# One attention tile's P.V on column strips of the array, and O transposed by VectorE

## The chip, the cores and the metric

The kernel runs on one core of one Trainium2 chip. Its time is the device time of one execution in microseconds (us). Three executions of the kernel before took 279.31, 279.51 and 279.59 us; their median, 279.51 us, is the time before. One execution was profiled: it took 279.08 us, of which its instructions span 277.4 us. TensorE, VectorE, ScalarE, GpSimd and the queue that issues most transfers, SyncE, appear in the profile as PE (weight loads as PEld), DVE, ACT, POOL and SP.

## What is computed

One transformer block with modulation by a condition `c`: sliding-window attention (16 heads of 28, window 256), then a gated MLP whose gate mixes along the sequence with the 2048x2048 matrix `w_sp`. All tensors are bfloat16, 2048 tokens of width 448. `ln` is layernorm without scale.

```python
mod = silu(c) @ w_mod                      # six vectors of 448: sa, ca, ga, sb, cb, gb
h = ln(x) * (1 + ca) + sa
q, k, v = split(h @ wqkv)                  # 16 heads of 28
s = q @ k.T * 28**-0.5                     # per head
s = where(0 <= i - j < 256, s, -1e9)       # query i, key j
x = x + ga * ((softmax(s) @ v) @ wo)
h = ln(x) * (1 + cb) + sb
z = gelu(h @ w_in); z1, z2 = z[:, :896], ln(z[:, 896:])
x = x + gb * ((z1 * (w_sp @ z2 + b_sp)) @ w_out)
```

## The kernel before

**How the order is made.** The program is a list of operations, each with its dependencies, made by the calls of `add`, `pe`, `dve`, `act`, `pool`, `turn` and `load`. Which engine does an operation, and in which order, is written out in the string `ORDER` (lines 19 to 74): a word such as `399.a.4.0` is operation 399, on ACT, with the buffers 4 and 0. Letters are p, a, v, g, s for PE, ACT, DVE, POOL and SP. `Sched` sets semaphore waits for what crosses engines (`waits`) and emits each engine's list (`emit`). Every engine works its own list strictly in order, so an operation that waits holds up all that stands behind it on its engine; SP's list holds nearly all DMA issues. A `Hold` is one use of a buffer; its `until` list says what has to be done before the buffer's next use.

**Stages.** (1) Loads, modulation vectors, norm and Q/K/V projections of the first block of four tiles (a tile is 128 tokens; blocks `tb` 0 to 3). Heads are padded from 28 to 32, so a group `qi` of four heads fills 128 partitions; Q and K lie transposed (`qT`, `KT`), V as `Vaug[128 keys, tile, head, 32]` with a column of ones at 28, so that P.V gives the sum of P as its column 28. (2) Attention of 16 query tiles `j`, each in two halves (two groups of four heads), with the projections of blocks 1 to 3 in between. (3) The projection by `w_in` with gelu; `w_sp` is read transposed meanwhile by DMA (`wspA`, `wspB`). (4) The product with `w_sp` and the output projection.

**Attention of a half, for tiles from 2 on.** The window of a query tile covers three key tiles: the oldest, the middle, the newest. Of the oldest and the newest each query needs a part. `S` (line 858) makes 36 small products with K=32, four heads at a time on four row strips of the array: first with 128 columns of weights, then sixteen with 64. They fill four PSUM banks (0 to 3), of which each head's 512 columns hold the middle tile of the first group and the two masked parts of both groups. `S mid` (line 867) is one product of 512 columns for the second group's middle tile, against `QBD`, Q spread block-diagonally (bank 5). ACT takes the exponential of both into `PW` (line 819: 2048 columns, then 512; five buffers). DVE multiplies with the 0/1 mask, once per group, from `PW` into another tile, `PT` (line 874). P.V (line 901) takes 128 keys x 128 queries of P as weights and 32 columns of V as moving operand: per half 24 products, into bank 4, where O has queries on partitions. Tiles 0 and 1 have one and two key tiles, go through lines 832 and 894, and use the same line 901.

**After P.V of a tile.** DVE takes the reciprocal of column 28 (line 915) and multiplies O with it into `o_sb` (line 917). SP issues a DMA that transposes `o_sb` into `hT` (`turn`, line 468). PE multiplies with `wo_g` (line 926), DVE adds to x (line 931), then `stats` (lines 592 to 600, the last step on POOL) and `norm` (lines 606 to 620: on POOL or DVE, with a small POOL operation, line 614, in front), a second DMA transposition, and the modulation (lines 949 and 951). The projection by `w_in` (lines 1011 and 1032) waits for these and for the last P.V.

Of the kernel before, what the change touches and what calls it, by code (L numbers as in the profile page):

```python
# [19 lines left out]
2.a 24.v 33.g 0.s 25.v 26.v 27.v 36.g 37.g 3.a 1.s 34.g 4.a 31.g 28.v 5.s 35.g 8.a 29.v 38.g 6.s 9.a 7.s 43.a 39.g 53.p.1 54.p.2 55.p.3 44.p.0 130.v  # L20
128.v 131.v 129.v 132.g 45.a 46.a 56.p.4 57.p.5 58.p.6 59.p.7 60.p.2 52.p.1 139.v 137.v 140.v 138.v 133.g 134.v 141.v 136.a.0 142.g 135.a.1 143.v
120.v 145.v.2 108.v 107.v 67.p.3 146.p.2 144.a.3 68.p.0 69.p.4 147.p 150.p.3 40.g 123.g 121.g 122.v 148.v 149.v 151.p 152.a 48.a 70.p.0 71.p.0
154.p.4.5.6.7 155.p 156.p 153.a 158.p 125.g 42.g 160.p 159.p 157.p 162.a 164.a 32.g 41.g 124.g 47.v 10.s 11.s 14.s 127.g 126.v 191.v 192.v 187.v 30.v
49.g 50.g 13.s 15.s 16.s 12.s 161.a 169.p.0 170.a 171.p.1 172.a 346.p.0 347.a.0 163.v 185.v 189.v 186.v 188.v 190.v 51.v 175.p.7 173.p.6 112.p.0
114.p.1 193.g 194.g 199.g 201.g 197.g 200.g.0 195.g 176.v 202.v.1 198.v.2 113.v 196.g.3 350.v 174.a 352.p.0 353.a.1 181.p.7 203.p.0 371.p.0 166.s
167.s 165.s 168.s 17.s 348.v 115.v 206.p.1 177.p.6 204.v 205.v 207.v 109.p.0 372.a.2 373.a 182.a 208.a 378.p.0 379.a.3 380.a 239.v 241.v 243.v 237.v
244.v 110.v 238.v 20.s 19.s 18.s 240.v 242.v 354.v 111.v 178.v 179.p.7 183.p.1 211.p.0 184.v 293.v 356.v 180.v 349.p.0 398.p.0 212.a 351.p 355.p
215.p.1 357.p 400.p.0 209.p.0 399.a.4.0 381.v 291.v 216.v 406.p.0 210.a 245.g 246.g 251.g 252.v.0 358.v 359.v.0 376.v 374.v 253.g 249.g 254.g.1 403.v
221.p.1 213.p.0 383.v 214.v 402.v 294.v 375.p.0 377.p 407.a.5.1 401.a 427.p.0 222.a 408.p.0 382.p 223.p.0 225.p.1 428.a.6.2 435.p.0 409.a 411.v
429.p.0 384.p 258.s 118.g 247.g 250.g.2 256.s 257.s 248.g.3 255.s 262.g 259.g 226.a 436.a.0.3 292.v 224.v 295.v 385.v 386.v.1 229.p.0 227.p.1 404.p.0  # L30
410.v 297.v 228.v 430.a 456.p.0 230.a 457.a.1.4 360.s 218.s 219.s 220.s 217.s 432.v 261.v 260.v 437.p.0 233.p.0 231.p.1 405.p 412.p 296.v 232.v 438.a
234.a 464.p.0 413.p 275.p.1 263.p.0 458.p.0 465.a.2.0 431.v 298.v 116.g 299.g 119.g 300.g 117.g 307.g 305.g 306.g.0 301.g 308.g.1 302.g.2 439.v 414.v
415.v.2 264.v 469.v 440.v 460.v 468.v 276.a 459.a 485.p.0 486.a.3.1 433.p.0 265.p.1 434.p 441.p 466.p.0 493.p.0 266.a 467.a 303.g 304.g.3 442.p
235.p.0 489.v 443.v 444.v.0 494.a.4.2 461.v 487.p.0 269.p.1 514.p.0 236.a 488.a 462.p.0 277.p.0 463.p 470.p 471.p 495.p.0 515.a.5.3 522.p.0 270.v
490.v 497.v 416.s 387.s 472.v 473.v.2 278.a 267.p.1 268.v 498.v 491.p.0 492.p 361.p.0 362.v 523.a.6.4 526.v 363.v 496.a 543.p.0 544.a.0.0 516.p.0
388.p.1 499.p 279.p.0 389.v 548.v 547.v 517.a 280.a 551.p.0 552.a.1.1 500.p 417.p.1 524.p.0 281.p.0 501.v 518.v 418.v 502.v.1 527.v 519.v 525.a 282.a
# [229 lines left out]
def bass_adaLN_cond__sliding_block__mixer_gmlp__prompt_kernel(  # L266
# [15 lines left out]
    NT = S // 128  # L282
    DC = 4
    DP = 512
    NB4 = NT // 4
    EPS = 1e-5
    SCALE = float(DH) ** -0.5
    NPT = 7
    NPW = 5

    ARENA_BYTES = 207 * 1024
    arena = nc.alloc_sbuf_tensor("arena", [128, ARENA_BYTES // 2], BF16)
    base = nc.lookup_mloc(arena).addr
    cursor = [0]
# [860 lines left out]
```

## Time and profile before

| | us |
|---|---|
| median of three executions | 279.51 (279.31 to 279.59) |
| the profiled execution | 279.08, of which 277.4 is its span |
| start to the first exponential of 2048 columns | 0 to 30.10 |
| from there to the end of the last exponential | 30.10 to 109.95 |
| from there to the first product with `w_sp` | 109.95 to 156.60 |
| the rest | 156.60 to 277.40 |

A table of busy times by stretch gives, per engine, the time in which it had an instruction under way, with the number of instructions in brackets. "idle before" in a group of instructions is the time the engine waited in front of them, and the name behind the arrow is what ended the wait. Matmuls overlap, so the mean duration of one is no price; the distance between starts is. The granted TensorE clock is 1.0 in every stretch.

### The profile page before, as it was taken

What the parts mean: (1) busy time and instruction counts of PE and PEld (TensorE: products, weight loads), DVE (VectorE), ACT (ScalarE), POOL (GpSimd) and SP (SyncE); (2) the same over time, 40 slices, a digit from 0 to 9 for tenths busy, and PEclk for the clock granted to TensorE, in tenths of its full rate; (3) what the DMA queues carried; (4) which work ended last, traced back from release to release, by engine and by line L of the source; (5) the groups of instructions that cost most, each with busy time, mean ns of one, the idle gap of its engine ahead of it and who ended that gap; (6) DMA issues with size and microseconds to landing.
All of it is one profiled execution on the core that took longest, in us unless ns stands there. A gap on an engine that the chain in (4) does not pass through costs nothing.

```text
span 277.4 us, 7383 instructions
## 1 busy us (share of the span) xinstructions
PE 266.4 (96%) x3198; PEld 140.8 (51%) x3225; DVE 164.4 (59%) x364; ACT 128.2 (46%) x154; POOL 127.2 (46%) x191
## 2 busy tenths in 40 slices
PE   4999999999999999999999999999999999999995
PEld 1636466656576766444444444444444444444452
DVE  5679999989989999679798300300320042025434
ACT  2587999999999999577676600000000000000000
POOL 6831826914725669884949000600571065334110
PEclk9999999999999999999999999999999999999999
DMA  7966142145993666834999999100000000001113
GB/s 208 304 170 205 23 91 47 21 80 96 121 225 79 80 80 97 194 77 83 190 176 205 206 197 187 35 0 0 0 2 0 0 0 2 0 0 56 62 50 99
DMA packets 65843, 26.01 MB, mean 94 GB/s; under 512 B 56466, under 2 KB 64723, under 8 KB 65811
## 3 DMA queue, kind: packets, MB, share of 16 engines
q1 hardware_dynamic: 65168, 24.68, 43.4%
q10 hardware_dynamic: 642, 0.86, 1.1%
q8 instruction: 25, 0.41, 0.6%
q14 instruction: 8, 0.06, 0.1%
HBM read 9.01 MB, written 1.84 MB: 39 GB/s over the span
## 4 chain that ended last, share of the span: by engine, by line
PE 82%; DVE 8%; DMA 4%; POOL 3%; issue 1%; ACT 0%; ACTq 0%; SPq 0%; POOLq 0%
PE ps L1055 35%; PE ps L1032 8%; PE ps L1072 7%; PE ps L1011 6%; PE ps L708 5%; PE ps L901 5%; PE ps L858 3%; DMA hT<-xn 3%; PE ps L926 3%; PE ps L756 3%; PE ps L867 2%; DVE st_all L592 2%; PE ps L557 1%; DMA c_row<-in_c_dram 1%; PE ps L696 1%; POOL hT L951 1%
## 5 line engine op out<-in xcount | busy, mean ns | idle before, releaser
L819 ACT ACTIVATE PW<-ps 128x2048 bf16<-128x2048 f32 (+1 forms) x56 | 67.4, 1242 | 2.9 <-PE ps L867 1.1
L1059 DVE TENSOR_TENSOR tmpg<-ps,bsp_bc 128x512 bf16<-128x512 f32 x28 | 19.1, 691 | 83.4 <-PE ps L1055 69.3
L1062 POOL TENSOR_TENSOR z1T<-tmpg,z1T 128x512 bf16<-128x512 bf16 x28 | 31.9, 1153 | 79.3 <-DVE tmpg L1059 79.3
L1055 PE MATMUL ps<-wspB,z 128*128 128x512 bf16 x218 | 49.5, 379 | 0.3
L1055 PE MATMUL ps<-wspA,z 128*128 128x512 bf16 x220 | 48.8, 379 | 0.3 <-issue 0.2
L874 DVE TENSOR_TENSOR PT<-PW,mask 128x1024 bf16<-128x1024 bf16 x56 | 38.9, 721 | 0.7 <-ACT PW L819 0.7
L1055 PEld LDWEIGHTS ps<-wspA,z 128*128 128x128 bf16 x224 | 21.8, 98 | 26.6 <-issue 0.4
L1055 PEld LDWEIGHTS ps<-wspB,z 128*128 128x128 bf16 x224 | 21.9, 98 | 26.2
L600 POOL TENSOR_TENSOR rs_all<-ve_all,neghalf 128x1 f32<-128x1 f32 (+2 forms) x37 | 23.6, 645 | 3.7 <-DVE ve_all L597 3.0
L1011 PE MATMUL ps<-w_in,hT 64*128 64x448 bf16 x224 | 23.0, 349 | 1.2 <-DVE hT L951 0.6
L901 PE MATMUL ps<-Vaug,PT 128*128 128x32 bf16 x496 | 24.1, 177 | 0.1
L901 PEld LDWEIGHTS ps<-Vaug,PT 128*128 128x128 bf16 x496 | 21.8, 96 | 4.0 <-DVE PT L894 0.6
L1032 PE MATMUL ps<-hT,w_in 64*128 64x512 bf16 x196 | 22.5, 376 | 0.0
L1072 PE MATMUL ps<-w_out_g,z1T 128*128 128x448 bf16 x112 | 22.2, 352 | 0.0
L708 PE MATMUL ps<-hT,WQK 128*128 128x512 bf16 x80 | 20.5, 379 | 1.3 <-issue 0.4
L616 POOL TENSOR_SCALAR xn<-x_sb,rs_all,ve_all 128x448 bf16<-128x448 bf16 x21 | 18.1, 863 | 7.0 <-DMA hT<-xn 6.4
L901 PE MATMUL ps<-Vaug,PW 128*128 128x32 bf16 x224 | 20.1, 176 | 0.0
L592 DVE BATCH_NORM_STATS2 st_all<-x_sb 128x6 f32<-128x448 bf16 x32 | 18.9, 610 | 1.6 <-DMA x_sb<-in_A_x_dram 1.5
L592 DVE BATCH_NORM_STATS2 st_all<-z 128x6 f32<-128x448 bf16 x32 | 18.3, 607 | 1.7 <-ACT z L1018 1.7
L901 PEld LDWEIGHTS ps<-Vaug,PW 128*128 128x128 bf16 x224 | 17.6, 96 | 1.9
L597 POOL TENSOR_SCALAR ve_all<-mv_all 128x1 f32<-128x1 f32 (+2 forms) x20 | 6.6, 334 | 25.1 <-DVE mv_all L595 21.5
L1018 ACT ACTIVATE z<-ps 128x896 bf16<-128x896 f32 x16 | 14.1, 916 | 7.8 <-PE ps L1011 6.8
(101 smaller groups left out, 343.9 us busy)
## 6 DMA issues: line engine op xcount, KB each, us to landing
out_dram<-fin SPq DMA_DIRECT2D x16, 112.0 KB, 1.7
x_sb<-in_A_x_dram SPq DMA_DIRECT2D x3, 448.0 KB, 3.9
wmod<-in_w_mod_dram SPq DMA_DIRECT2D x1, 1344.0 KB, 9.5
w_in<-in_B_w_in_dram SPq DMA_DIRECT2D x1, 1344.0 KB, 8.2
QBD<-qT SPq DMA_DIRECT2D x16, 64.0 KB, 2.5
w_out_g<-in_B_w_out_dram SPq DMA_DIRECT2D x1, 784.0 KB, 4.9
bsp_bc<-in_B_b_sp_dram SPq DMA_DIRECT2D x1, 512.0 KB, 5.0
x_sb<-in_A_x_dram SPq DMA_DIRECT2D x2, 224.0 KB, 4.2
```

Source lines behind the costliest of these rows:

```text
L592: st = [dve(0.62 if True else 0, lambda e, t=t, ci=ci, s=s: e.bn_stats(st_all[:, slot, t, ci, :], s()), deps(t), prio) for ci, s in enumer ...
L600: rs = pool(0.53 + 0.15 * len(tiles), lambda e: e.tensor_tensor(rs_all[:, slot, a:b], ve_all[:, slot, a:b], neghalf[:, 0:b - a], ALU.pow), ...
L708: m = pe(4 * MMS, [lambda e, h=h, g=g, kc=kc, tb=tb: e.matmul(ps[:, h.slot[0], :], lhsT=WQK[:, kc, 4 * g:4 * g + 4, :].rearrange("p a b -> ...
L819: ex = act(xdur, lambda e, out_ap=out_ap, in_ap=in_ap: e.activation(out_ap(), in_ap(), ACT.Exp, scale=SCALE), [s], v - 8.0 + u, takes, tab ...
L874: return dve(0.70, lambda e: e.tensor_tensor(cols(hp.slot[0] * 2048 + 1024 * k, [[256, 4], [128, 2], [1, 128]]), cols(at_w() + 128 + 192 * ...
L901: fns.append(lambda e, hp=hp, hO=hO, hi=hi, bi=bi, kb=kb, hd=hd, nb=nb, a=at[hi][bi], p_of=p_of: e.matmul(ps[:, hO.slot[0], 32 * hd:32 * h ...
L1011: return lambda e, kc, p0, start, stop: e.matmul(ps[:, hs[t % 2].slot[hf], 0:D], lhsT=hT[p0:p0 + 64, kc, t * 128:(t + 1) * 128], rhs=w_in[ ...
L1032: return lambda e, kc, p0, start, stop: e.matmul(ps[:, hs[b // 2].slot[b % 2], :], lhsT=w_in[p0:p0 + 64, kc, ft * 128:(ft + 1) * 128], rhs ...
L1055: m = pe(16 * MMS, [lambda e, h=h, si=si, ft=ft, tb=tb: e.matmul(ps[:, h.slot[0], :], lhsT=z2[:, si, ft * 128:(ft + 1) * 128], rhs=(wspA i ...
L1059: a = dve(0.7, lambda e, h=h, ht=ht, tb=tb: e.tensor_tensor(tmpg[:, ht.slot[0], :], ps[:, h.slot[0], :], bsp_bc[:, tb * 512:(tb + 1) * 512 ...
L1062: u = pool(1.16, lambda e, ht=ht, ft=ft, tb=tb: e.tensor_tensor(z1T[tb][:, ft, :], tmpg[:, ht.slot[0], :], z1T[tb][:, ft, :], ALU.mult), [ ...
L1072: return [lambda e, ft=ft: e.matmul(ps[:, h.slot[0], 0:D], lhsT=z1T[t // 4][:, ft, (t % 4) * 128:(t % 4 + 1) * 128], rhs=w_out_g[:, ft, :] ...
```

## The change

**P.V.** V is now the weights: 32 columns (a head) per column strip, four heads of a group side by side on the four strips of the array; P is the moving operand. O comes out with the head's 28 dimensions and its sum on partitions and queries along the columns. A half has 40 products: per group four with 128 columns (the middle tile) and sixteen with 64 (the four quarter-tiles of the oldest and newest keys).

**V in halves.** Since a product now takes 64 columns of P whose rows belong to half of one key tile and half of another, V is needed in that arrangement too: a new tile `VX` (two blocks x four arrangements x four tiles x 512). Two of the arrangements have one half of zeros. Per block four DMAs from `Vaug` fill it (64 partitions; 512, 256, 256 and 512 KB for a block of four tiles, half of that for the first), issued by SP; P.V of tiles 4tb to 4tb+3 waits for the four of block tb.

**S.** All 40 small products use 64 columns of weights, so eight can be in the array: per group two times four of 128 columns and two times four of 64, then two times four for the first group's middle tile.

**Mask.** One multiplication per half, in place in `PW`, 1024 elements per partition, on DVE or POOL. `PT` stays for tiles 0 and 1 alone and lies in `w_in`'s place, whose loads now wait for the P.V of those tiles.

**O.** DVE transposes bank 4 by 32x32 blocks into `ou` (float32), takes the reciprocal, multiplies on DVE or POOL into `o_sb`, and transposes that by 32x32 blocks into `hT`. The first DMA transposition of each tile is gone (16 of SP's). `wo` is loaded by four DMAs in the order of rows that this gives. `ou` lies in the last quarter of `wspA`, so ten of that tensor's sixteen loads wait for the last of these chains.

**Smaller edits.** POOL's operation of line 614 is gone for 28 norms. The first x load of tiles 2 and 3 is issued by ACT, and the loads of `w_mod` are issued in another order.

**The written order** is new as a whole. Read off the two strings:

| operation | before | after |
|---|---|---|
| masks | 64 DVE | 20 DVE, 12 POOL |
| O times reciprocal | 16 DVE | 9 DVE, 7 POOL |
| 32x32 transpositions | none | 32 DVE |
| evictions of K | 11 ACT, 5 DVE | 6 ACT, 10 DVE |
| evictions of Q | 9 ACT, 7 DVE | 11 ACT, 5 DVE |
| evictions of V | 10 ACT, 6 DVE | 9 ACT, 7 DVE |
| DMAs of SP for `VX` | none | 16 |

The diff, without the strings and cut to its core:

```diff
-    t_wo = load2("d_wo", "sp", 0.35, wo_g, ALL, A_wo, ALL, prio=-47.0)
+    t_wo = [load("d_wo%d" % h, "sp", 0.1, lambda e, h=h: e.dma_start(wo_g[32 * h:32 * h + DH, :, :], A_wo.rearrange("(g h d) n -> h d g n", h=4, d=DH)[h]), (), -47.0) for h in range(4)]
...
-        ve = ve_all[:, slot, t:t + 1]
-        nm = pool(0.34, lambda e: e.tensor_scalar(ve, m, z, -1.0, ALU.mult, ALU.mult), deps, prio)
-        op = add({"dve": (0.45, on_dve),
-                  "pool": (0.9, lambda e: e.tensor_scalar(to[:, h.slot[0], 0:D], x_sb[:, t, :], z, ve, ALU.mult, ALU.add))}, [nm], prio, [h])
+        op = add({"dve": (0.45, on_dve), "pool": (0.9, on_dve)}, deps, prio, [h])
...
+        for k, (fn, back) in enumerate((
+            (lambda e, vx=vx, vo=vo, a=a, b=b, n=n: e.dma_start(both(vx(0, 0), 8 * row, n), both(vo(0, a, b), 0, n)), 0),
+            (lambda e, vx=vx, vo=vo, a=a, b=b: e.dma_start(vx(0, 64), vo(0, a - 2, b - 2)), 2),
+            (lambda e, vx=vx, vo=vo, a=a, b=b: e.dma_start(vx(3, 0), vo(64, a, b)), 0),
+            (lambda e, vx=vx, vo=vo, a=a, b=b, n=n, row=row: e.dma_start(both(vx(1, 64), 8 * row, n), both(vo(64, a - 2, b - 2), 0, n)), 2))):
...
-                for place in (((0, m, 128, 0, 128, 0, 0),), ((k, o, 128, 0, 64, 128, 0) for k in range(2)), ((k, n, 128, 64, 128, 256, 0) for k in range(2)),
-                              ((k, *e) for k in range(2) for e in ((n, 64, 0, 64, 192, 0), (o + 64, 64, 64, 128, 192, 64)))):
+                for k in range(2):
+                    for key, lo, hi, col, p0 in ((n, 0, 128, 0, 0), (o + 64, 0, 128, 64, 64), (o, 0, 64, 0, 64), (n + 64, 64, 128, 128, 0)):
                         for t in range(4):
...
+                                ps[p0:p0 + 64, hm.slot[t], col:col + hi - lo], lhsT=KT[32 * t:32 * t + 32, qi, key:key + 64],
...
+                for p0 in (0, 64):
+                    for t in range(4):
+                        fm.append(lambda e, hm=hm, qi=qs[0], key=m + p0, p0=p0, t=t, j=j: e.matmul(
+                            ps[p0:p0 + 64, hm.slot[t], :].rearrange("p (a b) -> p a b", b=256)[:, :, 192:256], lhsT=KT[32 * t:32 * t + 32, qi, key:key + 64],
...
-                mks = [mask_all(k) for k in range(2)]
-                hw.until += mks
...
-                        fns.append(lambda e, hp=hp, hO=hO, hi=hi, bi=bi, kb=kb, hd=hd, nb=nb, a=at[hi][bi], p_of=p_of: e.matmul(
-                            ps[:, hO.slot[0], 32 * hd:32 * hd + 32], lhsT=p_of(a), rhs=Vaug[:, kb, hd, :],
-                            start=(bi == 0), stop=(bi == nb - 1)))
+                fk = lambda e, at_w=at_w, cols=cols: e.tensor_tensor(
+                    cols(at_w(), [[512, 4], [128, 4], [1, 64]], PW), cols(at_w(), [[512, 4], [128, 4], [1, 64]], PW),
+                    cols(0, [[0, 4], [64, 4], [1, 64]], mask3), ALU.mult)
+                mk = add({"dve": (0.72, fk), "pool": (2.2, fk)}, [exs[0]] + t_mk3, v - 7.0)
+                def parts(k, at_w=at_w, kbs=kbs, j=j):
...
+                    return [(Vaug[:, kbs[1]], mid, 0, 128), (vx(0), at(0), 0, 64), (vx(3), at(128), 64, 64),
+                            (vx(1), at(64), 0, 64), (vx(2), at(64), 64, 64)]
...
+                        fns.append(lambda e, hO=hO, hi=hi, qi=qi, V=V, of=of, q0=q0, w=w, first=bi == 0, last=bi == len(pieces) - 1: e.matmul(
+                            ps[32 * hi:32 * hi + 32, hO.slot[0], 128 * qi + q0:128 * qi + q0 + w], lhsT=V[:, 4 * qi + hi, :], rhs=of(hi),
+                            start=first, stop=last, tile_position=(0, 32 * hi)))
+            halves = [V_half[j // 4], t_vz[(j // 4) % 2]] if nb == 3 else []
...
-        rec = dve(0.25, lambda e, hO=hO, j=j, ov=ov: e.reciprocal(rec_all[:, j, :], ov(hO)[:, :, DH]), [lastPV], v - 9.0)
...
-        oe = turn("d_oT%d" % j, lambda j=j: hT[:, :, j * 128:(j + 1) * 128], lambda ho=ho: o_sb[:, ho.slot[0], :], [t_o, done], v - 9.0, tail=3.2 if j == NT - 1 else OTAIL)
+        ev = dve(0.69, lambda e, hO=hO, raw=raw: e.transpose(raw(), ps[:, hO.slot[0], :]), [lastPV, t_wqk], v - 9.0, [hu])
+        hO.until.append(ev)
+        rec = dve(0.25, lambda e, raw=raw, j=j, by_head=by_head: e.reciprocal(rec_all[:, j, :], by_head(raw())[:, :, DH]), [ev], v - 9.0)
+        fo = lambda e, raw=raw, even=even, j=j, by_head=by_head: e.tensor_tensor(by_head(even()), by_head(raw()), rec_all[:, j, :].unsqueeze(2).broadcast_to([128, H, 32]), ALU.mult)
+        mu = add({"dve": (0.62, fo), "pool": (1.35, fo)}, [rec], v - 9.0, [ho])
+        hu.until += [rec, mu]
+        oe = dve(0.62, lambda e, even=even, j=j: e.transpose(hT[:, :, j * 128:(j + 1) * 128], even().rearrange("p (g q) -> p g q", g=4)), [mu, done], v - 9.0)
...
+    for d in t_win_l:
+        d.deps.update(all_PV[:4])
```

293 lines of the change are left out of this document (150 added, 143 removed).

## The prediction, on record before the result was known

> **What bounds the kernel now.** I read the busy times by stretch first, cut at the first 2048-column exponential, the end of the last one and the first product with `w_sp`. Columns: length, then busy time of PE, PEld, DVE, ACT, POOL.
>
> ```profile
> 19.94:30.10 10.16, 10.11 (x174) 6.23 (x173) 9.57 (x25) 8.22 (x10) 4.05 (x10) 1.00 0.49 147
> 30.10:109.95 79.85, 78.09 (x1925) 50.85 (x1939) 75.64 (x156) 76.44 (x78) 46.03 (x65) 1.00 0.52 89
> 109.95:156.60 46.65, 45.54 (x453) 21.41 (x451) 38.08 (x104) 31.15 (x47) 31.64 (x60) 1.00 0.83 157
> 156.60:277.40 120.80, 117.34 (x550) 54.57 (x558) 28.43 (x44) 2.27 (x5) 32.86 (x29) 1.00 0.20 45
> ```
>
> PE is never short of work from 20 us on. But in the attention stretch (second line) PE leaves 1.8 us idle, ACT 3.4, DVE 4.2: three engines at 95 to 98%. A saving on one of them is worth only what the next allows. After the stretch PE alone counts.
>
> Then the chain of waits (start, length), for what PE's pieces cost, and the list of DMA issues (last figure: us to landing):
>
> ```profile
> 61.48 0.77 PE ps L926 x4
> ...
> 64.89 1.19 PE ps L901 x48
> 66.08 0.48 PE ps L858 x36
> 66.56 0.86 PE ps L926 x4
> ```
> ```profile
> hT<-o_sb SPq DMA_TRANSPOSE x16, 3.3
> wspA<-in_B_w_sp_dram SPq DMA_TRANSPOSE x16, 4.1
> ```
>
> P.V is 24.8 ns a product, a score batch 0.48 us; the same four products of line 926 take 0.77 us behind full-size work and 0.86 behind scores: 0.09 us for a change of tile shape.
>
> Then the groups of instructions within the attention stretch, and the timelines of DVE and POOL:
>
> ```profile
> L819 ACT ACTIVATE PW<-ps 128x2048 bf16<-128x2048 f32 (+1 forms) x56 | 67.4, 1242 | 2.9 <-PE ps L867 1.1 <-PE ps L858 1.1
> L874 DVE TENSOR_TENSOR PT<-PW,mask 128x1024 bf16<-128x1024 bf16 x54 | 37.6, 723 | 0.7 <-ACT PW L819 0.7
> ```
> ```profile
> 41.90 1.15 DVE L874 TENSOR_TENSOR PT<-PW,mask 128x1024 bf16<-128x1024 bf16 x1
> ```
> ```profile
> 41.46 1.04 POOL L576 TENSOR_TENSOR wo_g<-wo_g,gg_sb 128x448 bf16<-128x448 bf16 x1
> ```
>
> ACT's 67.4 us of exponentials are untouched by the change. A mask usually takes 0.68 us; this one took 1.15, and ended 0.55 us after the POOL instruction that was under way. Two others (47.90 us: 1.53; 67.12: 1.11) also ended 0.54 to 0.55 us behind a POOL instruction. So a two-input mask and POOL take turns.
>
> **The change part by part**, in the attention stretch, against 279.08 us.
>
> *P.V.* Before, 24 products x 24.8 ns = 0.59 us a half. Column strips are not in the trace; nearest are the row strips of the scores, where the starts of successive sets of four lie 65 ns apart with 128 columns and 29 ns with 64. A half: 2 x 65 + 8 x 29 ns = 0.36 us. Lower end, the issue alone, 80 instructions x 3.4 ns (spacing inside a set) = 0.27; upper end, no overlap, 8 x 56 ns (single 128-column products) + 32 x 25 ns (32-column ones) = 1.25. I take 0.36, four strips and the same columns: 28 x 0.23 = 6.4 us off PE, and 0.4 from tiles 0 and 1 (48 x 24.8 ns against 12 sets x 65 ns). The ends are -9.0 and +18.5 us.
>
> *Scores.* The sixteen 64-wide products of before run as eights, 53 ns apart. After: three eights of 128 columns and two of 64, 3 x 65 + 2 x 53 + 95 ns for the change of shape = 0.40 us against 0.48. With every eight at 53 ns it is 0.36; with fours in sequence (6 x 65 + 4 x 29 + 95 ns) 0.60. I take 0.40, the spacing seen for each width: -2.2 us, ends -3.4 and +3.4.
>
> *Changes of shape.* P.V now has a shape of its own, but the scores keep one instead of two. Counted in the written order: 93 before, 93 after. Nothing.
>
> One more Q/K projection (0.86) and output projection (0.77) fall into the stretch. PE: 78.1 - 6.8 - 2.2 + 1.6 = 70.7 us.
>
> *DVE.* Masks: 59 for 40.3 us become 17 x 0.68 = 11.6, -28.7. O: 14 transpositions from PSUM at 0.68 (row of the 128x512 eviction), 14 within SBUF at 0.60 (between the 128x512 modulation's 0.40 and 0.68, nearer the latter since every element is moved), 8 products at 0.62, less 15 of line 917 at 0.62 and one reciprocal: +13.3, ends +10 and +15. Moved in by the new order: evictions +3.8, statistics and norms of more tiles +5.9. Together 75.6 - 5.7 = 69.9 us.
>
> *ACT.* Evictions in the stretch fall from 22 (12.9 us) to 16 (9.3); neighbours overlap by 0.08 us: 76.4 - 3.1 = 73.3 us. ACT is now the longest of the engines; if it stays idle for 3.4 us as before, the stretch is 76.7 us: **-3.1**. With PE at 70.7, P.V and scores are off the path: up to 6.0 us that they lose costs nothing, and the next us all.
>
> *POOL.* Its 36.6 us of work (with each kind at its undisturbed duration: norm 0.71, modulation 0.77, line 614 0.26) become about 63: 12 masks at 2.2 (the two-input product on POOL takes 1.04 for 448 and 1.15 for 512 columns, so 2.1 to 2.3 for 1024), 6 products of O at 1.15, less 15 of line 614. The two-input work of DVE, which takes turns with it, falls from 39.0 (57 masks) to 16.6 us. The sum of both goes from 75.6 to about 80, above ACT's 76.7. What counts is POOL's last mask (first half of tile 13), with about 56 us of POOL and 13 of DVE's two-input work before it from 28 us on: it ends near 97 us, and its P.V stands right behind the scores of tile 14, due near 96. POOL sits in front of PE there: I add **+0.9**, between 0 (POOL ahead) and +3.4 (the whole excess).
>
> The Trainium skill (SBUF — State Buffer, section "SBUF: two separate sides") speaks against the change here: it says that a DVE operation with two SBUF inputs and a GpSimd operation lock the shared port pair in turn, for whole instructions. The three masks above agree; with every such wait at its full length the time would be the first rival's, 282.0.
>
> *V in halves.* 16 DMAs of SP, and two more for `wo` (10.8 us of issue at 0.6, as QBD's) take the place of 16 transpositions (20 us at 1.27), so SP has room. The queue: a block's 1.5 MB lands in about 9 us (1344 KB took 8.2), in front of it only transpositions. Covered, if the copies are issued two halves (5.5 us) or more ahead; if not, see the third rival.
>
> *Start.* Two V projections (0.77 each) go ahead of the first scores, one more Q/K projection ahead of tile 2's, one P.V (0.40) behind; the last modulation of block 0 stands behind a 0.91 us clear on DVE. PE was full there (10.11 of 10.16 us), but most of this work is only moved: **+0.3**, between -1.0 (earlier x load) and +1.5.
>
> *End.* Behind the last scores PE has one output projection less (0.77) and two more changes of shape. The chain of the last tile loses a DMA transposition (3.3 us) for two DVE operations of 1.28. But PE idles only 1.1 us in that stretch, so it gains at most that: **-0.8** in all, ends 0 and -1.5. The last stage does not change: `wspA`'s last load is issued by 148.9 and lands 4.1 later, 3.6 before use; it stands behind the same transpositions of x, so it moves with the stretch.
>
> Sum: -3.1 + 0.9 + 0.3 - 0.8 = -2.7, so 276.4 against the profiled 279.08. That execution lies 0.43 under the median: **276.8 us**.
>
> **Rivals.**
>
> *DVE waits for POOL (slower).* 25 two-input instructions of DVE remain while POOL holds the pair 63 of 77 us, now with instructions of 2.2. With half a (duration-weighted) instruction left, 0.65 us, each waits 0.82 x 0.65 = 0.53 us: 13 us, so DVE has 82.9 and the stretch is that long: +3.0 + 0.3 - 0.8, **282.0 us**. It decides from 0.4 us a wait: 69.9 + 10, and 1 idle, is 80.9. For: the rows above. Against: the same estimate gives 7.6 us for before, where the masks show 2.8 over 0.68; scaled so, 4.9 us, and DVE fits.
>
> *ACT runs without a gap (faster).* PE and DVE have slack, ACT's idle falls from 3.4 to 1.0 and POOL is in time: **273.5 us**. For: all of ACT's waits in the stretch are on PE. Against: POOL.
>
> *V's halves land late (slower).* The written order has block 2's four copies directly before the P.V that needs them. PE waits in its list, scores behind it, then ACT. 1.5 us in each of three blocks would be +4.5: **281.3 us**; it decides from 1.1 us each.
>
> *The strips don't overlap.* P.V at 1.25 us a half puts PE at 96.0, the stretch with its old idle at 97.8: **297 us**. In the Trainium skill (TensorEngine Tiling (Array Packing), Gotcha 2) column tiling excludes the fast weight load; no run shows 128-row strips, the 32x64 ones here start 3.4 ns apart, which speaks against the price.
>
> *Given back:* POOL's excess of 3.4 and the start eat ACT's saving, -3.1 + 3.4 + 0.3 - 0.8 = -0.2: **279.3 us**.
>
> **How the numbers follow.** Chances: forecast 0.35 (own range 275 to 279), ACT without a gap 0.25, DVE behind POOL 0.25, late halves 0.07, no overlap 0.03, given back 0.05. A change under 0.2% (0.56 us) can't be told from none here. Faster 0.35 + 0.25 = 0.60, same 0.05, slower 0.35. The range 272.0 to 282.5 leaves out a fifth of the second case, a third of the third, and most of the late halves and strips: 0.05 + 0.08 + 0.05 = 0.18.
>
> **What would show it.** Right: attention stretch near 77 us, ACT 95% busy, PE near 71, P.V near 0.36 us a half, POOL over 70 with its waits. Wrong: masks or products on DVE far over 0.68 us beside POOL; PE idle in front of P.V with DMA or POOL as its releaser; P.V over 0.6 us; a first exponential later than 22 us.

## The result, and the profile after

The changed kernel is slower: it took 300.15, 300.62 and 302.16 us, the kernel before 279.41 us in the median; the ratio is 1.077, interval 1.072 to 1.082. A fourth execution, disturbed, took 306.29 us and is left out below, where 300.6 us stands for the changed kernel, while the expectations quote 301.4, the median with it. Forecast were 276.8 us and a range from 272.0 to 282.5. The profiled execution took 300.62 us, its span is 298.3.

Busy times of the changed kernel by stretch, cut as before (length, then PE, PEld, DVE, ACT, POOL, granted clock, share of the DMA engines, GB/s):

```profile
25.94:35.11 9.17, 8.93 (x161) 5.06 (x159) 8.68 (x25) 7.07 (x8) 0.27 (x2) 1.00 0.43 120
35.11:130.79 95.68, 79.96 (x2480) 46.08 (x2482) 79.56 (x155) 74.87 (x73) 85.22 (x67) 0.96 0.62 126
130.79:177.21 46.42, 44.94 (x469) 22.46 (x465) 38.29 (x97) 30.11 (x45) 33.96 (x56) 1.00 0.72 124
177.21:298.30 121.09, 118.05 (x562) 54.72 (x560) 28.15 (x44) 2.50 (x6) 31.80 (x28) 1.00 0.22 47
```

The attention stretch takes 95.7 us instead of 79.8 (+15.8), the start 35.1 instead of 30.1 (+5.0); the two stretches behind are as before (-0.2 and +0.3). In the attention stretch no engine is near full any more: PE, 98% busy before, has 84%, VectorE 83%, ACT 78% instead of the 95% forecast; GpSimd, with 89%, is the busiest, and the first run below takes a tenth of its work away without effect. PE's idle time rises from 1.8 to 15.7 us, which is 14.0 of the 15.8; its busy time rises by 1.9. So time goes in waits. The chain of waits shows three kinds (start, length, what). First, at the start:

```profile
7.99 3.58 DMA wq_st<-in_A_wqkv_dram
...
11.61 5.83 DMA wq_st<-in_A_wqkv_dram
...
17.45 0.58 ACT WQK L596
```

ACT pads the query weights (line 596) piece by piece and waits for each piece's load, and it issues these two loads at 7.99 and 11.61 us; before, they went out at 2.35 and 2.83. Second, in the attention stretch, a wait for one of the new copies, and third, "issue":

```profile
55.57 6.62 DMA VX<-Vaug
...
62.23 0.53 PE ps L930 x40
```
```profile
85.53 0.13 PE ps L895 x2
85.67 2.00 issue
...
113.01 2.50 issue
```

"issue" is time in which PE waits for no semaphore. Here it stands in the middle of a batch of like products: seven such pauses over 0.25 us, the last just behind the stretch, sum to 8.2 us (before: none). Gaps between batches, where PE does wait for another engine or a transfer, sum to 7.1 us up to the last pause (before: 0.3).

A pause has a mark of its own in the trace's list of transfers. PE's instructions are fetched by transfers of 16 KB on a queue for instructions: 29 of them in the changed kernel, and 26 in a run below with 768 instructions of PE fewer. Before, 156 to 385 of PE's instructions lie between the starts of two fetches in the attention stretch, 256 in the mean. All but the last of the seven pauses lie in this table; "ahead" counts packets of 2 KB or more in the 4 us before the fetch's start:

| pause, us | last fetch | instructions since the fetch before | ahead | fetch's end to PE's resumption, us |
|---|---|---|---|---|
| 85.67 to 87.67 | 85.45 to 86.38 | 281 | 174 | 1.29 |
| 103.91 to 104.78 | 102.58 to 103.53 | 463 | 113 | 1.25 |
| 113.01 to 115.51 | 113.11 to 113.98 | 489 | 128 | 1.52 |
| 118.14 to 119.17 | 116.80 to 117.74 | 208 | 70 | 1.43 |
| 121.90 to 122.72 | 120.38 to 121.31 | 222 | 0 | 1.41 |
| 126.19 to 126.72 | 124.37 to 125.38 | 210 | 0 | 1.34 |

Every one of them ends 1.2 to 1.6 us after a fetch has ended, while the gaps between batches end 0.7 to 8.0 us after one; so I take it that PE had run out of instructions. The fetches themselves are no longer than before (0.88 to 1.49 us; before 0.89 to 1.62): they come late. All packets counted as "ahead" have 4 KB, a row of the V copies; no other transfer of the stretch has that size. The copies in the list of DMA issues:

```profile
VX<-Vaug SPq DMA_DIRECT2D x6, 512.0 KB, 5.4
VX<-Vaug SPq DMA_DIRECT2D x8, 256.0 KB, 4.7
```

In the groups of the stretch, masks and products of O on VectorE are longer than the 0.68 and 0.62 us forecast, and GpSimd's norm takes over twice its old 0.86 us:

```profile
L909 DVE TENSOR_TENSOR PW<-PW,mask 128x1024 bf16<-128x1024 bf16 x16 | 14.8, 925 | 1.9 <-ACT PW L847 1.7
L948 DVE TENSOR_TENSOR o_sb<-ou,rec_all 128x512 bf16<-128x512 f32 x8 | 9.1, 1140 | 0.1
L622 POOL TENSOR_SCALAR xn<-x_sb,mv_all,rs_all 128x448 bf16<-128x448 bf16 x16 | 30.8, 1934 | 0.4
L909 POOL TENSOR_TENSOR PW<-PW,mask 128x1024 bf16<-128x1024 bf16 x12 | 25.8, 2156 | 2.6 <-ACT PW L847 2.6
```

### The profile page after: what moved, and what is told of

Read it like the earlier page. It is cut to its first block, busy times and chain, and to the rows that moved or that the text cites. A ratio compares the mean times of both kernels' runs of the same rounds, so it can differ in the third digit from the quotient of the medians.

```text
span 298.3 us, 8519 instructions
## 1 busy us (share of the span) xinstructions
PE 271.0 (91%) x3785; PEld 137.4 (46%) x3785; DVE 170.9 (57%) x366; ACT 126.2 (42%) x148; POOL 164.5 (55%) x177
## 4 chain that ended last, share of the span: by engine, by line
PE 68%; DVE 10%; ACT 5%; DMA 5%; issue 4%; POOL 3%; SPq 3%; POOLq 0%
PE ps L1086 32%; PE ps L1103 7%; PE ps L719 6%; ACT PW L847 5%; PE ps L1063 4%; DVE st_all L605 4%; PE ps L930 4%; PE ps L955 3%; DMA wq_st<-in_A_wqkv_dram 3%; PE ps L1042 3%; PE ps L889 3%; PE ps L767 2%; DMA VX<-Vaug 2%; POOL xn L622 2%; PE ps L904 2%
## 5 line engine op out<-in xcount | busy, mean ns | idle before, releaser
L847 ACT ACTIVATE PW<-ps 128x2048 bf16<-128x2048 f32 (+1 forms) x56 | 68.0, 1237 | 18.8 <-PE ps L895 15.1
L622 POOL TENSOR_SCALAR xn<-x_sb,mv_all,rs_all 128x448 bf16<-128x448 bf16 x21 | 40.3, 1924 | 0.8
L719 PE MATMUL ps<-hT,WQK 128*128 128x512 bf16 x96 | 27.3, 419 | 2.6 <-POOL hT L672 1.3
L909 POOL TENSOR_TENSOR PW<-PW,mask 128x1024 bf16<-128x1024 bf16 x12 | 25.8, 2156 | 2.6 <-ACT PW L847 2.6
L1042 PE MATMUL ps<-w_in,hT 64*128 64x448 bf16 x224 | 22.2, 349 | 0.6 <-DVE hT L982 0.6
L1063 PE MATMUL ps<-hT,w_in 64*128 64x512 bf16 x196 | 21.8, 376 | 0.0
L610 POOL TENSOR_SCALAR ve_all<-mv_all 128x1 f32<-128x1 f32 (+2 forms) x22 | 5.2, 244 | 25.0 <-DVE mv_all L608 25.0
L1113 DVE TENSOR_TENSOR fin<-ps,x_sb 128x448 bf16<-128x448 f32 x16 | 9.6, 621 | 16.0 <-PE ps L1103 15.3
L1049 ACT ACTIVATE z<-ps 128x896 bf16<-128x896 f32 x16 | 14.1, 915 | 9.4 <-PE ps L1042 9.4
L1071 ACT ACTIVATE z1T<-ps 128x512 bf16<-128x512 f32 x28 | 14.5, 602 | 6.9 <-PE ps L1063 6.9
L719 PEld LDWEIGHTS ps<-hT,WQK 128*128 128x128 bf16 x96 | 9.3, 105 | 15.1 <-issue 3.3
L889 PE MATMUL ps<-qT,KT 32*64 32x64 bf16 (+1 forms) x896 | 11.6, 209 | 5.1 <-issue 4.3
```

The source lines that it names most:

```text
L622: on_dve = lambda e: e.tensor_scalar(to[:, h.slot[0], 0:D], x_sb[:, t, :], m, z, ALU.subtract, ALU.mult)
L719: m = pe(4 * MMS, [lambda e, h=h, g=g, kc=kc, tb=tb: e.matmul(ps[:, h.slot[0], :], lhsT=WQK[:, kc, 4 * g:4 * g + 4, :].rearrange("p a b -> ...
L847: ex = act(xdur, lambda e, out_ap=out_ap, in_ap=in_ap: e.activation(out_ap(), in_ap(), ACT.Exp, scale=SCALE), [s], v - 8.0 + u, takes, tab ...
L889: fm.append(lambda e, hm=hm, qi=qs[k], key=key, lo=lo, hi=hi, col=256 * k + col, p0=p0, t=t, j=j: e.matmul(ps[p0:p0 + 64, hm.slot[t], col: ...
L909: fk = lambda e, at_w=at_w, cols=cols: e.tensor_tensor(cols(at_w(), [[512, 4], [128, 4], [1, 64]], PW), cols(at_w(), [[512, 4], [128, 4], ...
L1042: return lambda e, kc, p0, start, stop: e.matmul(ps[:, hs[t % 2].slot[hf], 0:D], lhsT=hT[p0:p0 + 64, kc, t * 128:(t + 1) * 128], rhs=w_in[ ...
```

## The experiments

First theory: the V copies, which the prediction had priced at nothing, delay PE. Rivals: the slow norm on GpSimd with all that waits for it; the late start alone; GpSimd's masks, which hold up VectorE. All times below are medians of two to ten executions, with the kernel before between 279.3 and 280.3 us beside them. "Pauses" and "gaps" are sums over the attention stretch, as above.

### Three suspects, one by one and together

The old norm (one small operation more, then multiply and add instead of subtract and multiply):

```diff
-        op = add({"dve": (0.45, on_dve), "pool": (0.9, on_dve)}, deps, prio, [h])
+        if (slot, t) in ON_POOL:
+            ve = ve_all[:, slot, t:t + 1]
+            nm = pool(0.34, lambda e: e.tensor_scalar(ve, m, z, -1.0, ALU.mult, ALU.mult), deps, prio)
+            op = add({"pool": (0.9, lambda e: e.tensor_scalar(to[:, h.slot[0], 0:D], x_sb[:, t, :], z, ve, ALU.mult, ALU.add))}, [nm], prio, [h])
```

> One edit to the changed kernel: the 17 norms that POOL does take their old form again (multiply by rs, add -m*rs, with the small instruction that makes -m*rs in front). Theory A, the new form (subtract, multiply) is what made POOL's norm 1.92 us instead of 0.86: the norm falls to 0.7 to 0.9 us, POOL loses some 15 us of work in the attention stretch, the masks and products of DVE that wait behind it (1.5 to 2.6 us each) fall to 0.7 to 1.1 and the time falls by 5 to 9 us, to 292 to 296. Rival B, the norm is slow because of the more crowded port and not of its form: it stays near 1.9 us and the time within 2 us of 301. Rival C, PE is held by its own instruction supply and the late V copies: the norm gets fast, the time falls by less than 3 us.

Measured: 300.21 us (300.09 to 300.32), ratio 1.074 (1.061 to 1.087), stretch 95.8 us, pauses 8.1. The group of norms shows the form as the cause of their length:

```profile
L632 POOL TENSOR_SCALAR xn<-x_sb,rs_all,ve_all 128x448 bf16<-128x448 bf16 x21 | 18.3, 870 | 2.1
```

The norms take 22 us less of GpSimd, their small operations (21 x 0.32) 7 more, and the time is the same within its interval: the slow norm is real and hidden.

The loads of the query weights' second and third piece, issued by ACT straight behind its load of `w_mod`; neither they nor the other loads of query and key weights wait for x, as before the change (the list of smaller edits leaves this wait out):

```diff
-2.a 4.s 35.g 3.a 33.g
+2.a 4.s 35.g 3.a 8.a 9.a 33.g
...
-                    head("d_w%sc" % n, e, wq_st, A_wqkv, 3, 64, cols, -98.915 + 0.01 * k, land + 0.2, [t_x0[0]])]
+                    head("d_w%sc" % n, e, wq_st, A_wqkv, 3, 64, cols, -98.915 + 0.01 * k, land + 0.2)]
```

> One edit to the changed kernel: the two wq loads of ACT's list are issued straight after the loads of w_mod, and the four loads of wq that waited for x wait for nothing, as before the change. Theory A, the first exponential comes at 24.7 us instead of 19.9 because ACT issues the second of these loads only behind a copy that itself waits for the first: the first exponential comes at 19.5 to 21.5 us and the whole falls by 3 to 5 us, to 296 to 298. Rival: the start is bounded by PE's own work in the new order (two V projections more in front): the first exponential stays past 23 us, the time falls by less than 1.5.

Measured: 297.3 us (296.3 to 298.3), 3.3 less. The first exponential comes at 21.58 us instead of 25.94 (before: 19.94; the 24.7 of the expectation is the table load in front of it), the attention stretch stays at 97.0. The late issue of these loads, by their wait and their place together, is the cause of the late start.

The copies of blocks 1 to 3 left out (P.V reads the first block's arrangement):

```diff
-            halves = [V_half[j // 4], t_vz[(j // 4) % 2]] if nb == 3 else []
+            halves = [V_half[0], t_vz[0]] if nb == 3 else []
...
-                    vx = lambda k: VX[:, (j // 4) % 2, k, j % 4, :].rearrange("p (h d) -> p h d", d=32)
+                    vx = lambda k: VX[:, 0, k, 2 + j % 2, :].rearrange("p (h d) -> p h d", d=32)
```

> One edit to the changed kernel: the copies of V into VX are left out for blocks 1 to 3 (12 DMAs, 4.5 MB); the P.V of all tiles from 2 on reads the arrangement of block 0 instead, so tiles from 4 on compute with wrong V halves. Theory A, the copies' landing costs the wait in front of P.V near 60 us (2.2 us on PE, a gap of 5.8 us between exponentials) and little else: the time falls by 3 to 5 us, PE's pauses inside the score and P.V batches (8 to 9 us in all, named issue) stay over 6 us. Rival B, the pauses come from instruction fetches queued behind the copies: they fall below 3 us and the time falls by 8 us or more. Rival C, hidden: the time falls by less than 1.5 us.

Measured: 292.8 us (291.5 to 294.1), 7.8 us less; pauses 2.6 instead of 8.2, stretch 87.8. PE's busy time falls too, from 80.0 to 75.5 us: two spells at half clock, which the changed kernel has in this stretch (last section), are gone. So rival B had the pauses right, but they aren't all of it:

```profile
34.84:122.62 87.78, 75.53 (x2467) 44.85 (x2482) 81.12 (x155) 74.74 (x73) 84.79 (x66) 1.00 0.40 82
```

All three together (the first two edits compute the same as before, the third leaves the copies out):

> The three edits of the runs before together (old form of POOL's norm, wq loads early, no V copies for blocks 1 to 3, so the output of tiles from 4 on is wrong). If the three account for the loss: 277 to 284 us. If PE's pauses inside its batches are a cause of their own: 285 to 290 us with 8 us of them left in the attention stretch.

Measured: 284.55 us (284.0 to 285.1). 16.1 of the 21.2 us are in these three edits; 5 remain, and PE still has pauses of 2.2 and gaps of 3.6 us, and two spells at half clock (the stretch's clock is 0.96). At the longest gap, 1.3 us at 73 us, the chain goes through a mask of VectorE that lasts 2.00 us, and GpSimd has two masks under way from 71.12 to 75.76:

```profile
71.17 0.63 DVE x_sb L967
71.80 2.00 DVE PW L916
```

That mask ends at 73.80 us, 0.56 after the first of GpSimd's two.

### How the copies cost: by landing late or by traffic

The copies issued as before, but into memory that nobody reads:

```diff
-        vx = lambda k, p0, tb=tb, a=a, b=b: VX[p0:p0 + 64, tb % 2, k, a % 4:a % 4 + b - a].rearrange("p j c -> p (j c)")
+        vx = lambda k, p0, tb=tb, a=a, b=b: VX[p0:p0 + 64, min(tb, 1), k, a % 4:a % 4 + b - a].rearrange("p j c -> p (j c)")
...
-            halves = [V_half[j // 4], t_vz[(j // 4) % 2]] if nb == 3 else []
+            halves = [V_half[0], t_vz[0]] if nb == 3 else []
```

> The changed kernel with its twelve V copies of blocks 1 to 3 still issued, at their places, but into memory that nobody reads; P.V takes block 0's arrangement for all blocks, so no product waits for a copy after block 0 (the output is then wrong in its values). Leaving the copies out altogether gave 292.8 us and 2.6 us of pauses inside PE's batches, against 301.4 and 8.2. Theory A, the products wait for the copies to land: this run is like the one without copies, 291 to 295 us, pauses at most 3.5 us. Theory B, the copies' traffic delays PE's instruction fetches: pauses stay at 6 to 9 us and the time at 297 to 302 us; only the 2.2 us wait for a copy at 59.6 us can go.

Measured: 301.6 us (300.0 to 303.2), pauses 8.3. Nobody waits for a copy, and nothing is gained: theory B. Two spells at half clock are back, and PE's gaps over 0.25 us sum to 7.7 us, against 7.2 in the run without copies; so what the copies cost here lies in the pauses and the clock. The pauses look as before:

```profile
111.94 0.33 PE ps L891 x20
112.27 2.22 issue
```

Fewer small products, with the copies as they are:

```diff
                 unit(0, WMM, fm, need, 1.88, ...
+                if j > 3:
+                    fm = fm[:4] + fm[20:]
```

> The changed kernel with 16 of the 40 small score products of each half left out from tile 4 on (384 products; those columns keep older scores, so the output is wrong). Theory A, an instruction fetch is late because of the copies' packets, whatever PE consumes: pauses in PE's batches 7 to 9 us as before; the time falls by no more than the products' own 24 x 0.2 = 4.8 us, 296 to 300 us. Theory B, PE runs out because the many small products empty its instructions faster than they are fetched: pauses at most 5 us and 290 to 295.5 us.

Measured: 299.6 us (298.6 to 300.7): theory A's time, theory B's pauses (0.3 us). The gaps grew instead, from 7.1 to 16.1 us; PE now arrives at the products that need a copy before the copy does:

```profile
84.29 5.73 DMA VX<-Vaug
...
90.06 1.46 PE ps L932 x80
```

So the copies hold up PE twice, by late fetches and by late landing, and the two lie over each other: taking either away alone (this run and the one before it) gains 1 us at most, taking the copies away 7.8. Three waits for copies make 8.3 of the 16.1 us of gaps.

Is it the copies alone? The kernel before, whole, with twelve copies of V of the same sizes (the smaller ones 224 KB), each issued by SP behind the V that it copies, into dead memory:

```diff
+    for tb in (1, 2, 3):
+        for k, (fn, back) in enumerate((
+            (lambda e, vo=vo, two=two, a=a, b=b: e.dma_start(dead1[0:64], two(vo(0, a, b))), 0),
+            (lambda e, vo=vo, a=a, b=b: e.dma_start(dead2[64:128], vo(0, a - 2, b - 2)[:, 0:1792]), 2),
+            (lambda e, vo=vo, a=a, b=b: e.dma_start(dead2[0:64], vo(64, a, b)[:, 0:1792]), 0),
+            (lambda e, vo=vo, two=two, a=a, b=b: e.dma_start(dead1[64:128], two(vo(64, a - 2, b - 2))), 2))):
...
```

> The kernel before with twelve copies of V added, of the size and at the times of those of the changed kernel (blocks 1 to 3, 1.47 MB each), into memory that nobody reads. Its computation is whole. Theory A, the copies alone delay PE's instruction fetches: pauses of 4 us or more appear inside PE's batches in the attention stage (0 without them), 284 to 288 us. Theory B, the copies do harm only where PE's program is as dense as in the changed kernel (1,080 small score products and 1,128 of P.V in the stage): pauses below 1.5 us, 279 to 281 us. Where the time rises without pauses, other transfers (queries, normalised activations, weights) are late behind the copies.

Measured: 294.95 us (294.9 to 295.0) against 279.88, ratio 1.055 (1.048 to 1.061): more than either theory gave. The attention stretch takes 89.4 us instead of 79.8, the next one 52.0 instead of 46.6. Inside the stretch only 0.3 us of it is a pause; the chain goes over small transfers that the kernel before has, late behind the copies:

```profile
52.73 0.44 ACT Vaug L762
...
53.67 0.12 SPq L1100
...
53.83 0.61 SPq L1102
...
54.48 6.75 DMA hT<-o_sb
...
95.42 4.69 DMA QBD<-qT
```

The transposition of O usually lands 3.3 us after its issue, Q's spreading 2.5, so these are served late. But the first three lines show a second way: this transposition is also issued late. Its O was ready at 40.8 us (before: 40.2), and SP, which works its list in order, stood from 46.4 to 53.2 in front of a copy (line 1100) whose V ACT finished only then; before, the transposition went out at 46.4. PE's longest gap, 57.2 to 61.9, ends behind it. Behind the stretch PE waits 3.8 us, from 123.4, for another one that lands in 3.65 us but goes out 6.3 us after its O is ready (before: 3.2), and from 126.4 to 133.2 the clock is at half. So the copies do harm in a kernel that never waits for them; how much of the 15.1 us is their bytes and how much their place in SP's list, this run doesn't separate.

How much of it is in which copy? Like the first run of this section (copies that nobody reads), but with the two doubled copies (512 KB) of blocks 1 to 3 left out:

```diff
-                V_half[tb][-1].deps.update(V_half[tb - 1])
+                V_half[tb][-1].deps.update(V_half[tb - 1][1:3])
```

(and the words of those six copies out of the written order)

> Like the run whose copies nobody waits for (301.6 us, pauses 8.3 us), but with the two doubled copies (512 KB written each) of blocks 1 to 3 left out, so that only the two copies of 256 KB per block travel: a third of the bytes. P.V takes block 0's arrangement, as there. Leaving out all of them gave 292.8 us. Theory A, PE's fetches are delayed in proportion to the bytes queued: 294 to 297 us, pauses 3 to 5.5 us. Theory B, every copy costs, whatever its size: 298 to 302 us, pauses of 6 us or more.

Measured: 294.0 us (290.8, 294.0, 294.0), pauses 5.6, at the edge of theory A in both. The median falls by 7.6 us of the 8.8 that leaving out every copy gives, the profiled execution by 6.0 of 8.5. So two thirds of the bytes carry two thirds of the cost or more; whether their size counts or their number was not separated.

### Two ways to mend it

The old norm and the early loads with all copies:

> The changed kernel with the old form of the normalisation on GpSimd and the early loads of the query weights; the copies stay, all work is done. Theory A, the effects of the edits add (1.2 and 4.1 us): 294.5 to 297.5 us, and the attention stage stays at 93 us or more because of the copies. Theory B, GpSimd's freed 22 us help once the stage starts early: 294 us or less.

Measured: 293.8, 297.6 and 299.5 us; the profiled one, the fastest, has a stretch of 95.1 us, which theory A asked for (93 or more), though its time lies just inside theory B's. With such a spread the times alone don't decide.

The same with the doubled copies written by ScalarE, since they keep their partitions:

```diff
+            if k in (0, 3):
+                V_half.setdefault(tb, []).append(add({"act": (1.9, fn)}, [t_va, [V_ready[t] for t in range(a - back, b - back)], t_vz[tb % 2]], 40.0 * tb - 46.0))
+                continue
```

> The previous mended kernel (old normalisation, early loads, all work done) with the two doubled copies of each block, which keep their partitions, written by ScalarE instead of a DMA (8 operations of 64 x 2048 words, about 1.9 us each by the 2,048-column exponential). Theory A, the copies' bytes are what hurts: 288 to 292 us, pauses and gaps of PE in the stage together below 9 us (15.3 in the changed kernel). Theory B, the exponentials behind the copies in ScalarE's list come late instead: 293 to 297 us with a first 2,048-column exponential or a gap between exponentials later by over 4 us.

Measured: 295.1 us (294.3 to 295.3). Pauses fell to 2.1, gaps rose to 12.1: theory B. ACT, at 88.2 of 97.3 us, has become the busiest engine (the other four copies, line 798, take as long):

```profile
L795 ACT ACTIVATE VX<-Vaug 64x2048 f32<-64x2048 f32 (+1 forms) x4 | 6.8, 1694 | 0.1
```

Both are slower than the kernel before. No version with the new P.V and all its work done came near it.

### What the other 5 us are

From here on the three edits of 284.55 us are the base. GpSimd's twelve masks moved to VectorE (`.g` becomes `.v` in twelve words of the order; outputs of the runs from here on are wrong where copies, masks or scores are left out):

> The run with three edits (old form of the normalisation, early loads, no copies; 284.55 us) and in addition the twelve masks of GpSimd (2.16 us each) on VectorE, so that all masks run there. Theory A, what is left of the loss in the attention stage (85.5 us against 79.8) is P.V behind late masks and VectorE slowed beside GpSimd: 281 to 283.2 us, no VectorE mask over 0.9 us, gaps between PE's batches below 2.5 us. Theory B, VectorE is nearly full and 12 x 0.7 = 8.4 us more make it the bound: 285.5 to 289 us.

Measured: 291.5 us (289.6 to 293.4): theory B, and beyond its upper end. The stretch of the profiled one (293.4) is 93.0 us, at a clock of 0.94, which is three spells at half clock:

```profile
32.00:124.99 92.99, 81.44 (x2480) 45.99 (x2482) 78.98 (x167) 74.96 (x73) 48.16 (x72) 0.94 0.38 81
```

VectorE is at 85%, so it isn't full over the stretch; but its list is in order, and an eviction that PE needs stands behind a mask that waits for an exponential. The chain at the longest gap, 2.7 us at 73 us:

```profile
71.70 1.89 ACT PW L854
...
73.61 1.38 DVE PW L916
74.99 0.32 DVE hT L679
75.32 0.54 DVE Vaug L779
...
75.91 0.36 PE ps L962
```

In this order, masks on GpSimd are better than on VectorE.

The twelve masks left out altogether:

```diff
-            pv = pe(cost, fns, [mk, exs, lastPV, halves] + ...
+            pv = pe(cost, fns, [None if (j, half) in GONE else mk, exs, lastPV, halves] + ...
```

> The run with three edits (284.55 us: old normalisation, early loads, copies of blocks 1 to 3 left out) and the twelve masks of GpSimd left out besides, without a substitute (unmasked scores, so the output is wrong). Theory A, VectorE operations that last until a GpSimd mask ends (3.95 us of excess in that run, 2.0 instead of 0.6 us each in the chain) are on the path: 280 to 282.5 us, VectorE excess below 3.2 us. Theory B, they are hidden behind PE: 284 to 285.5 us.

Measured: 283.5 us (282.2 to 284.8, five executions), between the theories. VectorE operations over 0.1 us longer than the lower quartile of their kind are lengthened by 2.3 us in all instead of 6.9 (the 3.95 of the expectation counts only those that last until a GpSimd mask ends), and gaps fell from 3.6 to 2.1; no spell at half clock is left, but pauses rose from 2.2 to 5.2:

```profile
100.96 0.22 PE ps L896 x12
101.18 1.32 issue
...
104.97 0.25 PE ps L896 x15
105.22 1.01 issue
```

The fetches ahead of these two had no packet of 2 KB or more in front of them, and PE resumed 1.48 and 1.46 us after their ends. So the masks' cost seems covered by a next limit, the instructions themselves. New theory: PE's small products use its instructions up faster than they are fetched. Test: 16 small score products a half out (32 instructions with their weight loads), the large score product twice in their stead (2 instructions, about the same PE time):

```diff
+                if j > 3:
+                    fm = fm[:4] + fm[20:]
...
-                    rhs=QBD[...], start=True, stop=True)],
+                    rhs=QBD[...], start=True, stop=True)] * (2 if j > 3 else 1),
```

> The run with four edits (old normalisation, early loads, copies of blocks 1 to 3 and GpSimd's twelve masks left out; 282.2 to 284.8 us, 5.2 us of pauses in PE's batches) and, from tile 4 on, 16 of the 40 small score products of each half left out and the one large score product issued twice in their stead: 30 instructions of PE fewer per half at about the same PE time (16 small ones 0.2 us, the large one 0.21 us). Scores are then wrong. Theory A, the pauses are PE out of instructions because small products use them up faster than they are fetched: pauses below 1.5 us and the time 2.5 to 4.5 us below the run beside it. Theory B, the pauses have another cause that the count of instructions does not touch: pauses of 4 us or more, time within 1 us.

> The run with four edits once more, beside e13_fewer on the same chip: 282.2 to 284.8 us as before under both theories, with 4 to 6 us of pauses in PE's batches.

Measured on one chip: 277.9 us (277.1 to 279.4) against 284.1 (282.3 to 286.0). Pauses 0.7 against 5.3 us, PE's time in products (by distances between starts) 75.9 against 76.7:

```profile
30.23:110.36 80.13, 75.75 (x2120) 41.86 (x2122) 72.26 (x155) 73.97 (x73) 48.08 (x72) 1.00 0.46 90
```

Theory A, by more than it had forecast: 6.2 us for 720 instructions of PE fewer; 4.6 of it are pauses, and the products account for 0.9. (The first exponential of a half can also start 0.2 us earlier, since the large product stands behind the small ones.)

## Why the prediction was wrong

**The step that failed is "V in halves"**: "SP has room ... Covered", a cost of nothing. It asked whether SP could issue the copies and whether they would land in time, and not what travels beside 1.5 MB a block. Without the copies the kernel is 7.8 us faster. Copies of the same sizes make the kernel before 15.1 us slower, there in part because SP's list stands still in front of a copy whose V isn't ready; "SP has room" had counted issue time alone. The third rival (halves land late, chance 0.07) had the place right and the mechanism half: the wait at 60.0 us (2.2 us) is one, but with nobody waiting for copies nothing is gained. The larger part came as pauses in batches that need no copy, through PE's fetches, and as two spells at half clock.

**The number of PE instructions had no step at all.** The prediction priced PE by spacing. By spacing P.V came out right: 0.46 us a half in the chain, which is the 0.36 forecast and the 0.09 for the change of shape; over the stretch P.V fell from 19.3 to 14.1 us, 5.2 of the 6.4 forecast (distances between starts, waits over 10 ns taken out). But 2,480 products stand where 1,925 stood, and with the copies and masks gone 5.2 us of pauses remain that fewer instructions remove. The Trainium skill (Runtime: NRT & Kernel Launch, "Instruction fetch mechanics") says that fetching in 16 KB blocks is mostly hidden, since a sequencer dispatches more slowly than blocks arrive. The 16 KB blocks agree with the transfers here; that they are hidden does not hold for PE in this kernel.

**Scores were mis-sized.** Forecast 0.40 us a half for 0.48; measured 0.49 to 0.51 (0.31 for 32 products, 0.18 to 0.20 for eight), in the stretch 14.7 instead of 13.1 us: +1.6 where -2.2 stood (13.9 in the run without GpSimd's masks, whose clock never falls). In undisturbed halves the first four eights start 80, 28 and 60 ns apart, 168 in all for the 183 forecast; what was missed lies behind the fourth, 97 ns for 53, and behind the fifth and last, 226 ns to the next product for 160. PE came to 80.0 us, forecast 70.7; besides these, the Q/K projections are in it, 17.9 us where 14.0 and one more (0.9) had been counted, and two spells at half clock (last section). It wasn't PE's work that set the end, though: PE was idle for 15.7 us.

**The start was mis-sized**: +0.3 forecast (up to +1.5), +5.0 measured. The prediction counted work on PE there and not that ACT's loads of the query weights now wait for x and go out 5.6 and 8.8 us later, with ACT's padding behind them; issuing them early took 4.4 us off the first exponential.

**DVE and POOL.** DVE came to 79.6 us for 69.9. Operations over 0.1 us longer than the lower quartile of their kind make 9.9 us of that (3.4 before), 6.7 of it beside GpSimd's masks and products of O and 1.8 beside its products on `wo_g`; the prediction had put 0.9 us (at most 3.4) on the stretch for it. So the mechanism of the first rival (282.0 us) was at work, and the rule cited of the Trainium skill (SBUF — State Buffer, "SBUF: two separate sides") agrees with the 2.00 us mask above. That it set the end was not shown: without the masks the time fell by about 1 us, within the spread of these runs. POOL came to 85.2 us for 63, for the new form of the norm (1.93 us against 0.71), which the prediction took to cost what the old one did; this changed nothing in the time. The 63 was a slip besides: the terms named for it, 36.6, 12 masks, 6 products and 15 small operations less, give 66.0.

**Right** were ACT's work (74.9 us against 73.3) and the transpositions by VectorE within 0.1 us (0.71 and 0.69 against 0.68 and 0.60); the end was nearly so (-0.2 and +0.3 us in the two stretches behind, forecast -0.8). Of the signs that the prediction named, PE idle in front of P.V with DMA as releaser, masks far over 0.68 us and a first exponential later than 22 us all came. PE idle with no releaser was not among them.

Of the 21.2 us lost, the early loads alone give back 3.3, leaving out the copies alone 7.8, both with the norm 16.1. Behind the last 5 stand PE's lack of instructions, which a run shows to be a limit, spells at half clock, and VectorE's waits beside GpSimd, which are shown to be there but not to set the end. How much each would be alone was not settled. Nor is it settled whether a late fetch is requested late or served late; the trace has only its start and end.

## What to carry to other kernels

A transfer that nobody waits for is not free: ask what else travels at that time, PE's instructions and small transfers in the chain among it, and price a copy by running it into dead memory. Look also at what stands behind it in the issuing engine's list while it waits for its source. Count instructions as well as time when a change cuts products into smaller ones: here a score batch and its P.V use up 160 instructions in about 1 us, a fetch brings some 256, and "issue" inside a batch of like products is the sign. Where several covers lie over each other, as late landing, late fetches and late masks did here, taking one away can show nothing; take them away together, then put each back.

## What was not expected of the hardware

**Instruction fetches can bound PE.** Pauses of 0.3 to 2.5 us, which end 1.2 to 1.7 us after the end of a 16 KB fetch, in every run with the new P.V; 8.2 us in the changed kernel, 0.3 to 0.7 with 16 small products a half fewer. That PE lacked instructions there is inferred from these ends and from that run; no row of the trace names it.

**A short idle can halve PE's clock for one window.** PE was idle from 60.0 for 2.23 us; the granted clock fell to 0.50 from 63.6 to 67.0:

```profile
60.20:63.60 3.40, 1.37 (x83) 1.07 (x84) 0.72 (x2) 0.31 (x1) 3.40 (x3) 1.00 0.53 64
63.60:67.01 3.41, 3.41 (x36) 1.28 (x38) 2.01 (x4) 2.38 (x3) 3.12 (x4) 0.50 0.44 77
67.01:70.00 2.99, 2.99 (x117) 1.73 (x105) 1.82 (x3) 2.41 (x3) 2.59 (x3) 1.00 0.12 27
```

The same followed the pause at 85.7 (2.00 us), not the one at 113.0 (2.50 us). Both spells last 3.4 us, the length of the window that the Trainium skill gives (TensorE: Matmul & The Clock Gate, "Part 1: The HAM clock gate"), so PE, busy throughout the first, lost half of it, 1.7 us. The page has the clock fall after at least one idle window; here PE had work in part of every window of that length, and the measurement decides. So a wait costs more than its length where it draws such a window. Which idle does is not settled: one of 2.30 us at 76.4 in the run without copies drew none, and in the run with three edits a spell at 107.9 came behind idles of 0.56 and 0.65 us.

**GpSimd's norm depends on its form.** Subtract then multiply takes 1.86 us for 128x448 (median), multiply then add 0.72 us. The two forms also read one scalar from different tiles (`mv_all` or `ve_all`), so whether it is the order of the operations alone was not tested.
